# 186 products of the last chunks as two halves of 64 contraction rows, ordered by a semaphore

## The chip, the cores and the metric

The kernel runs on one core of a Trainium2 chip. The metric is device time in microseconds, the median of several runs. Work is done by TensorE (matrix products into the accumulation memory, PSUM), VectorE, ScalarE and GpSimd (elementwise work), and by DMA queues. In the profile they are PE, DVE, ACT, POOL and SP; PEld is TensorE's weight load.

## The reference

Windowed attention with block summaries, then a two-layer network with an ELU between the layers. All of it is in f32.

```python
# attention: q, k, v of (4, 8, 768, 64); 24 blocks of 32 keys; window 16
k_sum = k.reshape(B, H, nb, block, D).max(axis=3)
v_sum = v.reshape(B, H, nb, block, D).mean(axis=3)
scores = [scale * q @ k.T where |i - j| < 16, scale * q @ k_sum.T + log(32)]
a = softmax(scores);  attn = a @ [v, v_sum]
x = attn as (3072 tokens, 512)
# network: w_in (512, 2048), w_out (2048, 512)
h = x @ w_in
g = where(h > 0, h, exp(min(h, 0)) - 1)
out = g @ w_out
```

## The kernel before, in words

The 3072 tokens go in six chunks of 512. A chunk's first layer is 16 blocks of 128 hidden columns, its second layer adds the 16 blocks into four PSUM banks of 128 tokens by 512. Each f32 operand is split into a high and a low part (both float32r), so a product of two f32 matrices is three products on TensorE: high by high, high by low, low by high. "Product" below means one such instruction: a stationary operand of 128 contraction rows by 128 columns and a moving one of 128 rows by 256 or 512 columns.

The change lies in the last two chunks. There the first layer of the last chunk is done by a scheme with seven block products in place of eight (numbered 1 to 7, function `run` inside the loop over eight pairs of hidden blocks, `i` = 0 to 7, `then` holds what is done with each result). Each of the seven takes six TensorE products of 512 columns into one bank (line 788, `seventh`). In the same loop the second layer of the chunk before goes on (`layer2`, line 642).

After that the second layer of the last chunk is done in the same manner (`run_pair`, line 1162, with its products in line 868): seven pairs of hidden blocks, 0 to 6, each of 42 products of 256 columns, six to a block product. Products 1, 6, 7 and 5 have a bank each (`m`, four banks, two token blocks side by side in it). Products 2, 3 and 4 add into the four banks `o`: 2 into the lower columns of the first two, 3 into the upper columns of the same two, 4 into the lower columns of the last two. All seven pairs add into the same places. The order within a pair is 1, 6, 7, 5, 2, 3, 4. Beside it, VectorE and ScalarE prepare the operands of a later pair (`prepare`, `parts`): `token_wholes` adds and subtracts, `token_blocks` (ScalarE line 839, VectorE line 830) and `token_halves` (line 855) split into high and low parts. They have two sets of homes, so the operands for pair i + 2 go where those of pair i lay, and their first write waits for the last product of pair i that reads them.

The order of the instructions on each engine is that in which the code is written out here, one stream an engine. TensorE takes its stream in order; an instruction that waits for a semaphore holds back those behind it.

Of the kernel before, what the change touches and what calls it, by code (L numbers as in the profile page):

```python
# [7 lines left out]

# [2 lines left out]

# [15 lines left out]
P = 128  # L27
# [11 lines left out]
def attn_elu_ffn(ctx: ExitStack, tc: tile.TileContext, qT, kT, vT, v, w_in, w_out, out):  # L39
    nc = tc.nc  # L40
# [10 lines left out]
    NF = DF // P  # L51
# [143 lines left out]
    def x_of(c, part, p):  # L195
        return xs[c][part][p // 2][:, p % 2, :]
# [403 lines left out]
    def fetch(f, tag):  # L600
        weights[(2, f)] = wts.tile([P, 2, WC], F32R, tag=tag, name="w2")
        nc.sync.dma_start(out=weights[(2, f)].bitcast(F32), in_=kept[f])

    def layer1(c, f):
        w = weights[(1, f)]
        h_ps = psum.tile([P, CH], F32, tag="h", name="h", bufs=2)
        parts = ((0, 0), (0, 1), (1, 0))
        runs = [(cc, part) for cc in range(NCC) for part in parts]
        if c == 0:
            runs = [r for r in runs if r[1][0] == 0] + [r for r in runs if r[1][0] == 1]  # L610
        for k, (cc, (a, bb)) in enumerate(runs):
            nc.tensor.matmul(h_ps, w[:, a, cc * P:(cc + 1) * P], x_of(c, bb, cc), start=(k == 0), stop=(k == len(runs) - 1))  # L612
        return h_ps
# [164 lines left out]
    def seventh(i, k, bank):  # L778

        left, right = LEFT[k], RIGHT[k]  # L780
        if left[0] == "a":
            tile, at = weights[(1, 2 * i + int(left[1]) - 1)], 2 * int(left[2]) - 2
        else:
            tile, at = sums_of[i][left]
        runs = [(cc, part) for cc in range(2) for part in ((0, 0), (0, 1), (1, 0))]
        for j, (cc, (a, bb)) in enumerate(runs):
            moving = xs[4][bb][int(right[1]) - 1] if right in ("b11", "b21") else pair[right][bb]
            nc.tensor.matmul(bank, tile[:, a, (at + cc) * P:(at + cc + 1) * P], moving[:, cc, :],  # L788
                             start=(j == 0), stop=(j == len(runs) - 1))

    inner = {}

# [66 lines left out]
    def layer2_seventh(i, k, outs, first, last):  # L859

        left = inner["left", i][k]
        one, two = inner[i]
        low, high = slice(0, WC // 2), slice(WC // 2, WC)
        w1, w2 = (weights[(2, 2 * i + j)] for j in range(2))
        w, cols = {1: (w1, low), 2: (w2, low), 3: (w2, high), 4: (two, low), 5: (one, low), 6: (two, high), 7: (one, high)}[k]
        for s in range(2):
            for j, (a, bb) in enumerate(((0, 0), (0, 1), (1, 0))):
                nc.tensor.matmul(outs[s], left[a][:, s * P:(s + 1) * P], w[:, bb, cols],  # L868
                                 start=first and j == 0 and k != 3 and (s == 0 or k in (2, 4)), stop=last and j == 2 and s == 1)

    def begin_next():

# [90 lines left out]
    with tc.manual_schedule(engines={engines["PE"], engines["SP"]}):  # L963
# [4 lines left out]
        for n in range(NF, 4 * NF):  # L968
# [11 lines left out]
            for b, first in first_at.items():  # L980
                steps = [i for i in range(first - 9, first) if i % NF > 0][:2 * NP]
                if n in steps:
                    i, p = divmod(steps.index(n), NP)
# [76 lines left out]
        for i in range(NF // 2):  # L1060
            p1, u2, u3, u4, e22, e12 = flat[:6]

            def first(ps):
                nc.scalar.copy(out=p1, in_=ps)

            def second(ps):
                add(ps, ps, p1)
                e = exp_of(ps)
                elu(e, ps)
                split(late - 1, 2 * i, e)  # L1070

            def sixth(ps):
                add(u2, ps, p1)

            def last(ps):
                add(u3, ps, u2)

            def fifth(ps):
                add(u4, ps, u2)
                add(ps, ps, u3)  # L1080
                finish(e22, ps)

            def third(ps):
                add(ps, ps, u4)
                finish(e12, ps)

            def fourth(ps):
                add(ps, ps, u3)
                e = exp_of(ps)
                elu(e, ps)  # L1090
                split(late - 1, 2 * i + 1, e, low=nc.vector if i == NF // 2 - 1 else None)

            then = {1: first, 6: sixth, 5: fifth, 2: second, 7: last, 3: third, 4: fourth}

            def run(*ks):
                for k in ks:
                    tag, bufs = (("h", 2), ("a0", 1), ("h", 2), ("a1", 1))[n_seventh[0] % 4]
                    n_seventh[0] += 1
                    ps = psum.tile([P, CH], F32, tag=tag, name="h", bufs=bufs)
                    seventh(i, k, ps)  # L1100
                    then[k](ps)

            if i == 0:
                run(1, 2)
                fetch(0, "w2_0")
                layer2(3, NF - 1)
                fetch(1, "w2_1")
                run(6, 7, 5, 3)
                fetch(2, "w2_4")
                fetch(3, "w2_5")  # L1110
                layer2(late - 1, 0)
                run(4)
            else:
                turn = gs["hi"]
                store(i - 1, 0, e12)
                store(i - 1, 1, e22)
                if i == NF // 2 - 2:
                    fetch_g(0)
                if i == NF // 2 - 1:
                    fetch_inner(0, [(wts, "w2_2"), (wts, "w2_3")])  # L1120
                    fetch_g(1)
                    run(1, 6, 7)
                    with tc.issue_after(turn):
                        list(parts(0))
                    run(5, 2)
                    layer2(late - 1, 2 * i - 1)
                    run(4, 3)
                else:
                    run(1, 6, 7, 5, 2)
                    layer2(late - 1, 2 * i - 1)  # L1130
                    run(3, 4)
                layer2(late - 1, 2 * i)
            if i + 1 < NF // 2:
                weight_sums(i + 1)
            for j in range(2 if i < 6 else 0):
                fetch(2 * i + 4 + j, f"w1_{2 * i + j}")
            if i in last_models:
                m = last_models[i]
                wholes[m] = [ffn.tile([P, WC], F32, tag="cv", name="one", bufs=2) for _ in range(2)]
                for part in range(2):  # L1140
                    model_sums(m, part, *(weights[(2, 2 * m + j)] for j in range(2)))
                model_halves(m, [(att, "xa2"), (att, "xa3")])
                model_store(m)
# [6 lines left out]
    with tc.manual_schedule(engines=set(engines.values())):  # L1150
        ends = (NF - 2, NF - 1)

        def prepare(i):
            list(parts(i))

        half_m = DO // 2
        o_acc[late] = [psum.tile([P, DO], F32, tag=tag, name="o", bufs=bufs) for tag, bufs in (("h", 2), ("h", 2), ("a1", 1), ("a0", 1))]
        outs = {}
        for k, (s, cols) in {2: (0, 0), 3: (0, 1), 4: (2, 0)}.items():
            outs[k] = [o_acc[late][s + j][:, cols * half_m:(cols + 1) * half_m] for j in range(2)]  # L1160

        def run_pair(i, ks=(1, 6, 7, 5, 2, 3, 4)):
            for k in ks:
                layer2_seventh(i, k, outs[k], i == 0, i == NF // 2 - 2 and k not in (2, 3, 4))

        run_pair(0, (2, 4))
        with tc.issue_after(gs["hi"]):
            prepare(1)
        layer2(late - 1, NF - 1)
        banks = {k: psum.tile([P, 2, half_m], F32, tag=f"o{j}", name="m") for j, k in enumerate((1, 6, 7, 5))}  # L1170
        outs.update((k, [t[:, s, :] for s in range(2)]) for k, t in banks.items())
        run_pair(0, (3, 1, 6, 7, 5))
        fetch_g(4)
        fetch_inner(4, [(wts, "w2_0"), (wts, "w2_1")])
        for i in (5, 6, 7):
            fetch_g(i)
        run_pair(1)
        prepare(2)
        fetch_inner(5, [(wts, "w2_2"), (wts, "w2_3")])
        run_pair(2)  # L1180
        prepare(3)
        fetch_inner(6, [(wts, "w2_6"), (wts, "w2_7")])
        run_pair(3)
        prepare(4)
        run_pair(4)
        prepare(5)
        run_pair(5)
        prepare(6)
        for j, f in enumerate(ends):
            split(late, f, g_tiles[NF // 2 - 1][j], wts.tile([P, 2, CH], F32R, tag=f"w1_{12 + j}", name="g"))  # L1190
        run_pair(6)
        shared = [wts.tile([P, 2, DO], F32, tag=f"w2_{4 + j}", name="shared") for j in range(2)]
        m1, u4, u3, v3 = (shared[j][:, :, k * half_m:(k + 1) * half_m] for j in range(2) for k in range(2))
        nc.scalar.copy(out=m1, in_=banks[1])
        add(u3, banks[6], m1)
        add(u4, banks[5], u3)
        add(u3, banks[7], u3)
        add(v3, banks[5], u3)
        layer2_last(late, ends, shared)
# [37 lines left out]
```

## Time and profile before

| | |
|---|---|
| median of 3 runs | 603.74 us (603.58 to 604.01) |
| span of the profiled execution | 601.7 us |
| busy: TensorE | 591.7 us, 98% |
| busy: VectorE, ScalarE, GpSimd | 382.6, 341.5, 346.7 us |
| products of line 868 (256 columns) | 294 |
| products of line 788 (512 columns) | 336 |

The span runs from the first to the last instruction of one execution; the timed runs hold some 2 us more around it. In the timeline a row gives the start and the length of a run of like instructions on one engine. A product's length is modelled and overlaps that of the next: the pitch, from start to start, is what a product takes of TensorE's time.

### The profile page before, as it was taken

Reading aid. Unit: us, or ns where it says so; the run is one execution under the profiler, and the core shown is the slowest. Engines: PE = TensorE matmul, PEld = TensorE weight load, DVE = VectorE, ACT = ScalarE, POOL = GpSimd, SP = SyncE. Lnnn points to the kernel's source line nnn. Section 1 sums busy time; section 2 is a strip of 40 time slices with the busy share of each in tenths; the row PEclk is TensorE's granted clock in tenths of the full one; section 3 lists DMA queues with packets and bytes.
Section 4 is the critical chain, followed back from the end, with each engine's and each line's share of the span. In section 5 each row is a group of like instructions: output and inputs, shape, how many; then the busy total and the mean of one; then the engine's idle time right before and its main releaser. Section 6 shows DMA issues by size and latency. Waiting matters only on the chain.

```text
span 601.7 us, 11834 instructions
## 1 busy us (share of the span) xinstructions
PE 591.7 (98%) x4134; PEld 488.9 (81%) x4134; DVE 382.6 (64%) x1078; ACT 341.5 (57%) x849; POOL 346.7 (58%) x368
## 2 busy tenths in 40 slices
PE   8899999999999999999999999999999999999997
PEld 7678778878888788888887888878888888888997
DVE  7767766647566665657774655666685444459773
ACT  5787777865554345553555645555556555555340
POOL 5778888883332333546578893322668779991001
PEclk9999999999999999999999999999999999999999
DMA  9999979307466566645976565552365233536951
GB/s 328 230 285 308 308 231 296 98 1 272 130 192 214 173 215 217 181 132 174 272 217 214 188 201 178 173 172 73 106 213 171 104 107 103 182 153 243 377 202 71
DMA packets 90092, 115.90 MB, mean 193 GB/s; under 512 B 31409, under 2 KB 67505, under 8 KB 90033
## 3 DMA queue, kind: packets, MB, share of 16 engines
q1 hardware_dynamic: 87296, 110.29, 58.4%
q10 hardware_dynamic: 2736, 4.85, 2.2%
q8 instruction: 33, 0.54, 0.4%
q14 instruction: 27, 0.21, 0.1%
HBM read 88.11 MB, written 26.21 MB: 190 GB/s over the span
## 4 chain that ended last, share of the span: by engine, by line
PE 84%; DMA 7%; DVE 4%; ACT 1%; SPq 1%; issue 1%; POOL 1%; DVEq 0%; POOLq 0%
PE o L642 32%; PE h L612 25%; PE h L788 11%; PE m L868 3%; PE o_ps L175 3%; PE s L543 2%; PE o L868 2%; DMA raw_w<-in_w_out_dram 2%; PE s L366 2%; DMA vw<-vs 1%; DMA vw<-in_v_dram 1%; DMA qbd<-in_qT_dram 1%; DMA n<-in_kT_dram 1%; PE o L677 1%; PE idle L303 1%
## 5 line engine op out<-in xcount | busy, mean ns | idle before, releaser
L612 PE MATMUL h<-x,w 128*128 128x512 f32 x768 | 188.7, 394 | 0.0
L630 POOL TENSOR_TENSOR gl<-e,gh 128x512 fp32r<-128x512 f32 x79 | 102.2, 1294 | 127.3 <-ACT gh L629 87.9
L612 PEld LDWEIGHTS h<-x,w 128*128 128x128 f32 x768 | 141.7, 188 | 31.5 <-issue 2.4
L642 PE MATMUL o<-w,gh 128*128 128x512 f32 x640 | 164.7, 392 | 0.0
L642 PEld LDWEIGHTS o<-w,gh 128*128 128x128 f32 x640 | 118.9, 188 | 26.0 <-ACT gh L629 0.8
L623 DVE SCALAR_TENSOR_TENSOR e<-e,h 128x512 f32<-128x512 f32 x80 | 54.9, 686 | 58.9 <-ACT e L619 55.0
L618 ACT ACTIVATE e<-h 128x512 f32<-128x512 f32 x80 | 47.4, 593 | 75.1 <-PE h L612 66.5
L642 PE MATMUL o<-w,gl 128*128 128x512 f32 x320 | 88.1, 389 | 0.8 <-POOL gl L630 0.8
L571 DVE STREAM_TRANSPOSE pt<-sm 32x256 f32<-32x256 f32 x192 | 83.7, 436 | 4.2 <-POOL sm L162 1.5
L153 ACT ACTIVATE sm<-sm,mx 128x120 f32<-128x120 f32 x192 | 73.2, 383 | 19.8 <-DVE mx L145 19.5
L162 POOL TENSOR_TENSOR sm<-sm,r 128x480 f32<-128x480 f32 x48 | 47.8, 996 | 58.0 <-DVE r L161 38.4
L629 ACT CAST gh<-e 128x512 fp32r<-128x512 f32 x80 | 49.6, 619 | 55.0 <-DVE e L623 53.4
L642 PEld LDWEIGHTS o<-w,gl 128*128 128x128 f32 x320 | 60.0, 188 | 13.7 <-POOL gl L630 1.2
L619 ACT ACTIVATE e<-e 128x512 f32<-128x512 f32 x80 | 50.6, 632 | 2.1
L129 POOL TENSOR_TENSOR w<-cv,w 128x512 fp32r<-128x512 f32 x32 | 41.3, 1290 | 5.5 <-ACT w L127 2.6
L145 DVE CUSTOM_DVE_ANT_0 sm<-s,mask 128x120 f32<-128x120 f32 x192 | 41.2, 276 | 0.4 <-PE s L366 0.4
L153 ACT ACTIVATION_READ_ACCUMULATOR sm<-sm,mx 128x1 f32 x192 | 35.9, 187 | 0.0
L120 DVE SCALAR_TENSOR_TENSOR sh<-sh,raw_w 128x512 uint32<-128x512 uint32 x32 | 22.3, 697 | 19.7 <-POOL w L129 9.8
L788 PE MATMUL h<-t,sums 128*128 128x512 f32 x144 | 33.9, 389 | 0.0
L788 PEld LDWEIGHTS h<-t,sums 128*128 128x128 f32 x144 | 27.0, 188 | 5.6
L123 DVE SCALAR_TENSOR_TENSOR cv<-raw_w,sh 128x512 uint32<-128x512 uint32 x32 | 22.0, 688 | 10.9 <-POOL w L129 9.8
L175 PEld LDWEIGHTS o_ps<-pt,vw 120*64 120x64 f32 x640 | 20.6, 137 | 8.5 <-issue 6.0
(147 smaller groups left out, 783.9 us busy)
## 6 DMA issues: line engine op xcount, KB each, us to landing
w<-kept SPq DMA_DIRECT2D x48, 512.0 KB, 4.1
raw_w<-in_w_in_dram SPq DMA_DIRECT2D x16, 512.0 KB, 5.6
raw_w<-in_w_out_dram SPq DMA_DIRECT2D x16, 512.0 KB, 4.2
kept<-w SPq DMA_DIRECT2D x16, 512.0 KB, 3.4
inner<-model SPq DMA_DIRECT2D x14, 512.0 KB, 6.0
model<-inner SPq DMA_DIRECT2D x12, 512.0 KB, 7.1
qbd<-in_qT_dram SPq DMA_DIRECT2D x32, 128.0 KB, 2.8
out_dram<-ots ACTq DMA_DIRECT2D x16, 256.0 KB, 3.9
```

Source lines behind the costliest of these rows:

```text
L129: nc.gpsimd.tensor_tensor(out=w[:, 1, :], in0=cv, in1=w[:, 0, :].bitcast(F32), op=ALU.subtract)
L153: nc.scalar.activation(out=sm[:, t, :], in_=sm[:, t, :], func=AF.Exp, bias=mx[:, t, :], scale=-1.0, accum_out=z[:, t, 0:1])
L162: nc.gpsimd.tensor_tensor(out=sm, in0=sm, in1=r.broadcast_to([P, UW, KC]), op=ALU.mult)
L571: nc.vector.transpose(pt2[j * BLK:(j + 1) * BLK, :, a * BLK:(a + 1) * BLK], sm2[a * BLK:(a + 1) * BLK, :, j * BLK:(j + 1) * BLK])
L612: nc.tensor.matmul(h_ps, w[:, a, cc * P:(cc + 1) * P], x_of(c, bb, cc), start=(k == 0), stop=(k == len(runs) - 1))
L618: nc.scalar.activation(out=e, in_=h_ps, func=AF.Relu, scale=-1.0)
L619: nc.scalar.activation(out=e, in_=e, func=AF.Exp, scale=-1.0)
L623: top = nc.vector.scalar_tensor_tensor(out=e, in0=e, scalar=-1.0, in1=h_ps, op0=ALU.add, op1=ALU.max)
L629: gs["hi"] = nc.scalar.copy(out=gh, in_=e).ins
L630: last = (low or nc.gpsimd).tensor_tensor(out=gl, in0=e, in1=gh.bitcast(F32), op=ALU.subtract)
L642: nc.tensor.matmul(o_acc[c][s], a[:, s * P:(s + 1) * P], w[:, bb, :], start=first and f == 0, stop=last and f == NF - 1)
L788: nc.tensor.matmul(bank, tile[:, a, (at + cc) * P:(at + cc + 1) * P], moving[:, cc, :], start=(j == 0), stop=(j == len(runs) - 1))
```

## The change

A product of 128 contraction rows is sent as two products of 64 rows, an upper half (rows 0 to 63) and a lower half (rows 64 to 127), which add into the same place of the same bank. The lower half is issued eight products behind its upper half: first eight or so upper halves, then upper and lower in turn, and at the end the eight lower halves left. So while both are under way they work on different banks. Where one kind of half opens a run of products in a bank, it waits for a semaphore that the other kind raised at the end of its run there; the semaphore is TensorE's own.

It is done at two places: for block products 1, 6 and 7 of pair 4 of the first layer (18 products of 512 columns), and for pairs 1 to 4 of the second layer (168 products of 256 columns), through which the lag runs on without a break. The order of the seven in a pair of the second layer is now 1, 6, 7, 5, 2, 4, 3.

```diff
+    row_sem = tc.alloc_semaphore("rows")
+    signalled = [0]
+    waiting, told = [], {}
+    def half_rows(item, r, again):
+        o, left, right, first, last, begins, ends = item
+        rows = slice(r * (P // 2), (r + 1) * (P // 2))
+        made = nc.tensor.matmul(o, left[rows], right[rows], start=first and r == 0, stop=last and r == 1)
+        bank = o.tensor.name
+        if begins and (bank, 1 - r) in told:
+            made.wait_op(row_sem, told[bank, 1 - r], "sem-ge")
+        if ends and (r == 0 or again):
+            nc.tensor.drain(fusable=True).then_inc(row_sem, 1)
+            signalled[0] += 1
+            told[bank, r] = signalled[0]
+    def by_halves(items, lag, end, after=None):
+        banks = [item[0].tensor.name for item in items]
+        new = [n == 0 or banks[n] != banks[n - 1] for n in range(len(items))] + [True]
+        items = [(*item, new[n], new[n + 1]) for n, item in enumerate(items)]
+        for item in items + (lag * [None] if end else []):
+            if item:
+                half_rows(item, 0, after is None)
+                waiting.append(item)
+            if len(waiting) > lag or not item:
+                done = waiting.pop(0)
+                half_rows(done, 1, after is None)
+                if after and done[-1]:
+                    after.pop(0)()
...
-                    run(1, 6, 7, 5, 2)
+                    run(1, 6, 7, rows=i == 4)
+                    run(5, 2)
...
-        def run_pair(i, ks=(1, 6, 7, 5, 2, 3, 4)):
+        def run_pair(i, ks=(1, 6, 7, 5, 2, 4, 3)):
...
+        def run_rows(i, end=False):
+            by_halves(run_pair(i), 8, end)
-        run_pair(1)
+        run_rows(1)
         prepare(2)
...
-        run_pair(4)
+        run_rows(4, True)
         prepare(5)
-        run_pair(5)
+        whole(run_pair(5))
```

`seventh` and `layer2_seventh` now return a list of products, which `whole` issues as before. `run` hands the list and the follow-up of each block product to `by_halves` where `rows` is set. `drain(fusable=True).then_inc` puts the signal on the product before it where that one carries none yet. In the built program there are 83 signals: 74 stand on a product, and 9 are drain instructions of their own, behind a product that already carries TensorE's signal to the other engines (two of the nine at the very end of pair 4's lower halves).

TensorE at the start of the first place, before: `h_5715` is the bank of product 1, `h_5723` that of product 6 (numbers tell buffers apart).

```order
L788 MATMUL h_5715<-x_3730,w1_8_1258 128x512 [waits DVE_49]
L788 MATMUL h_5715<-x_3732,w1_8_1258 128x512
L788 MATMUL h_5715<-x_3730,w1_8_1258 128x512 x2
L788 MATMUL h_5715<-x_3732,w1_8_1258 128x512
L788 MATMUL h_5715<-x_3730,w1_8_1258 128x512
L788 MATMUL h_5723<-t2_4587,sums_5703 128x512 [waits DVE_49]
L788 MATMUL h_5723<-t2_4588,sums_5703 128x512
L788 MATMUL h_5723<-t2_4587,sums_5703 128x512 x2
L788 MATMUL h_5723<-t2_4588,sums_5703 128x512
L788 MATMUL h_5723<-t2_4587,sums_5703 128x512
```

And in the changed kernel, where line 614 is the half product and `h_5716` the bank of product 6:

```order
L614 MATMUL h_5715<-x_3730,w1_8_1258 128x512 [waits DVE_49]
L614 MATMUL h_5715<-x_3732,w1_8_1258 128x512
L614 MATMUL h_5715<-x_3730,w1_8_1258 128x512 x2
L614 MATMUL h_5715<-x_3732,w1_8_1258 128x512
L614 MATMUL h_5715<-x_3730,w1_8_1258 128x512
L614 MATMUL h_5716<-t2_4587,sums_5703 128x512 [waits DVE_49]
L614 MATMUL h_5716<-t2_4588,sums_5703 128x512
L614 MATMUL h_5716<-t2_4587,sums_5703 128x512
L614 MATMUL h_5715<-x_3730,w1_8_1258 128x512 [waits rows]
L614 MATMUL h_5716<-t2_4587,sums_5703 128x512
L614 MATMUL h_5715<-x_3732,w1_8_1258 128x512
L614 MATMUL h_5716<-t2_4588,sums_5703 128x512
```

Nine upper halves go ahead; the first lower half of product 1 stands as the tenth, waits for `rows`, and from there upper and lower halves alternate.

TensorE in pair 1 of the second layer, before: the last of product 5 (`m_6332`), then product 2 into banks `o_6277` and `o_6278`, and product 3 into the upper columns of the same two.

```order
L868 MATMUL m_6332<-model_6260,sums_6303 128x256 x2
L868 MATMUL m_6332<-model_6260,sums_6304 128x256
L868 MATMUL m_6332<-model_6260,sums_6303 128x256 x2
L868 MATMUL m_6332<-model_6260,sums_6304 128x256
L868 MATMUL o_6277<-w2_5292,sums_6297 128x256 x2
L868 MATMUL o_6277<-w2_5292,sums_6298 128x256
L868 MATMUL o_6278<-w2_5292,sums_6297 128x256 x2
L868 MATMUL o_6278<-w2_5292,sums_6298 128x256
L868 MATMUL o_6277<-w2_5292,sums_6303 128x256 x2
L868 MATMUL o_6277<-w2_5292,sums_6304 128x256
L868 MATMUL o_6278<-w2_5292,sums_6303 128x256 x2
L868 MATMUL o_6278<-w2_5292,sums_6304 128x256
```

And in the changed kernel, where those two banks are `o_6298` and `o_6299`, `m_6353` is product 5's bank and `o_6301` a bank of product 4; `sums_6318` and `sums_6319` belong to product 2, `sums_6324` and on to product 3:

```order
L614 MATMUL o_6300<-model_6282,sums_6319 128x256
L614 MATMUL o_6298<-w2_5292,sums_6318 128x256 [waits rows]
L614 MATMUL o_6301<-model_6282,sums_6318 128x256
L614 MATMUL o_6298<-w2_5292,sums_6318 128x256
L614 MATMUL o_6301<-model_6282,sums_6318 128x256
L614 MATMUL o_6298<-w2_5292,sums_6319 128x256
L614 MATMUL o_6301<-model_6282,sums_6319 128x256
L614 MATMUL o_6299<-w2_5292,sums_6318 128x256 [waits rows]
L614 MATMUL o_6298<-w2_5292,sums_6324 128x256 [waits rows]
L614 MATMUL o_6299<-w2_5292,sums_6318 128x256
L614 MATMUL o_6298<-w2_5292,sums_6324 128x256
L614 MATMUL o_6299<-w2_5292,sums_6319 128x256
```

The first upper half of product 3 into `o_6298` waits for `rows`, and stands three instructions behind the last lower half of product 2 into that bank.

## Rows read from the trace of the kernel before

**Rows 1.** The page: its head, TensorE's busy time, granted clock, the chain's shares

```profile
span 601.7 us, 11834 instructions
...
PE 591.7 (98%) x4134; PEld 488.9 (81%) x4134; DVE 382.6 (64%) x1078; ACT 341.5 (57%) x849; POOL 346.7 (58%) x368
...
PEclk9999999999999999999999999999999999999999
...
PE 84%; DMA 7%; DVE 4%; ACT 1%; SPq 1%; issue 1%; POOL 1%; DVEq 0%; POOLq 0%
```

**Rows 2.** Who TensorE waited for, 480 to 602 us: total us, times, longest

```profile
PE o L868 <- DVE vw L623: 0.2, 1, 0.2
```

**Rows 3.** Timeline of TensorE, 494.4 to 500.2 us: start us, length us

```profile
494.46 1.52 PE L788 MATMUL h<-x,w 128*128 128x512 f32 x6
495.82 4.24 PE L788 MATMUL h<-t,sums 128*128 128x512 f32 x18
499.90 0.62 PE L788 MATMUL h<-x,w 128*128 128x512 f32 x2
```

**Rows 4.** Timeline of TensorE, 567.3 to 572.7 us

```profile
567.58 0.88 PE L868 MATMUL m<-w,sums 128*128 128x256 f32 x6
568.30 2.32 PE L868 MATMUL m<-model,sums 128*128 128x256 f32 x18
570.46 1.60 PE L868 MATMUL o<-w,sums 128*128 128x256 f32 x12
571.90 0.88 PE L868 MATMUL o<-model,sums 128*128 128x256 f32 x6
572.62 0.28 PE L868 MATMUL m<-w,sums 128*128 128x256 f32 x1
```

**Rows 5.** Groups of TensorE instructions by shape: count, busy us, mean ns

```profile
L788 PE MATMUL h<-t,sums 128*128 128x512 f32 x144 | 33.9, 389 | 0.0
...
L543 PE MATMUL s<-kw,qbd 64*64 64x120 f32 x512 | 16.8, 269 | 0.9 <-DVE x L202 0.9
L868 PE MATMUL m<-model,sums 128*128 128x256 f32 x126 | 16.3, 283 | 0.0
...
L533 PE MATMUL s<-kw,qbd 128*128 128x120 f32 x64 | 8.6, 277 | 0.5 <-DVE x L202 0.5
```

**Rows 6.** Timeline of TensorE, 135.4 to 136.3 us

```profile
135.19 0.59 PE L543 MATMUL s<-kw,qbd 64*64 64x120 f32 x16
135.71 0.96 PE L612 MATMUL h<-x,w 128*128 128x512 f32 x3
```

**Rows 7.** Timeline of TensorE, 97.9 to 99.0 us

```profile
98.04 1.05 PE L533 MATMUL s<-kw,qbd 128*128 128x120 f32 x8
```

**Rows 8.** Timeline of all engines, 567.3 to 568.2 us

```profile
567.46 0.79 PEld L868 LDWEIGHTS m<-w,sums 128*128 128x128 f32 x6
...
567.70 0.93 ACT L839 CAST sums<-g 128x256 fp32r<-128x256 f32 x2 [2.52 <-PE o L868]
```

**Rows 9.** Timeline of TensorE, 554.2 to 556.3 us

```profile
555.38 0.98 PE L868 MATMUL o<-model,sums 128*128 128x256 f32 x6 [0.19 <-DVE vw L623]
556.20 0.40 PE L642 MATMUL o<-w,gh 128*128 128x512 f32 x1
```

**Rows 10.** Timeline of VectorE, 567.3 to 572.7 us

```profile
568.14 1.22 DVE L830 TENSOR_TENSOR sums<-g,sums 128x256 fp32r<-128x256 f32 x2 [0.23 <-ACT sums L839]
569.61 1.23 DVE L830 TENSOR_TENSOR sums<-pt,sums 128x1024 fp32r<-128x1024 f32 x1 [0.26 <-ACT sums L855]
```

More of the change, by code (lines that the diff above doesn't have):

```diff
@@ L10 @@
 from contextlib import ExitStack
+from functools import partial
 import concourse.bass as bass
@@ L602, in fetch, with whole @@
         nc.sync.dma_start(out=weights[(2, f)].bitcast(F32), in_=kept[f])
+    row_sem = tc.alloc_semaphore("rows")
[25 more added lines that the diff above has]
+                    after.pop(0)()
+    def whole(items):
+        for o, left, right, first, last in items:
+            nc.tensor.matmul(o, left, right, start=first, stop=last)
     def layer1(c, f):
@@ L785, in seventh @@
         runs = [(cc, part) for cc in range(2) for part in ((0, 0), (0, 1), (1, 0))]
+        items = []
         for j, (cc, (a, bb)) in enumerate(runs):
             moving = xs[4][bb][int(right[1]) - 1] if right in ("b11", "b21") else pair[right][bb]
-            nc.tensor.matmul(bank, tile[:, a, (at + cc) * P:(at + cc + 1) * P], moving[:, cc, :],
-                             start=(j == 0), stop=(j == len(runs) - 1))
+            items.append((bank, tile[:, a, (at + cc) * P:(at + cc + 1) * P], moving[:, cc, :], j == 0, j == len(runs) - 1))
+        return items
     inner = {}
@@ L865, in layer2_seventh @@
         w, cols = {1: (w1, low), 2: (w2, low), 3: (w2, high), 4: (two, low), 5: (one, low), 6: (two, high), 7: (one, high)}[k]
[L866 to L869, printed above, removed]
+        return [(outs[s], left[a][:, s * P:(s + 1) * P], w[:, bb, cols],
+                 first and j == 0 and k != 3 and (s == 0 or k in (2, 4)), last and j == 2 and s == 1)
+                for s in range(2) for j, (a, bb) in enumerate(((0, 0), (0, 1), (1, 0)))]
     def begin_next():
@@ L1093, in attn_elu_ffn, with run @@
             then = {1: first, 6: sixth, 5: fifth, 2: second, 7: last, 3: third, 4: fourth}
-            def run(*ks):
+            def run(*ks, rows=False):
+                products, after = [], []
                 for k in ks:
@@ L1099, in run @@
                     ps = psum.tile([P, CH], F32, tag=tag, name="h", bufs=bufs)
-                    seventh(i, k, ps)
-                    then[k](ps)
+                    items = seventh(i, k, ps)
+                    if rows:
+                        products += items
+                        after.append(partial(then[k], ps))
+                    else:
+                        whole(items)
+                        then[k](ps)
+                if rows:
+                    by_halves(products, 8, True, after)
             if i == 0:
@@ L1160, in attn_elu_ffn @@
             outs[k] = [o_acc[late][s + j][:, cols * half_m:(cols + 1) * half_m] for j in range(2)]
-        def run_pair(i, ks=(1, 6, 7, 5, 2, 3, 4)):
-            for k in ks:
-                layer2_seventh(i, k, outs[k], i == 0, i == NF // 2 - 2 and k not in (2, 3, 4))
-        run_pair(0, (2, 4))
+        def run_pair(i, ks=(1, 6, 7, 5, 2, 4, 3)):
+            return [item for k in ks for item in layer2_seventh(i, k, outs[k], i == 0, i == NF // 2 - 2 and k not in (2, 3, 4))]
+        whole(run_pair(0, (2, 4)))
         with tc.issue_after(gs["hi"]):
@@ L1171, in attn_elu_ffn @@
         outs.update((k, [t[:, s, :] for s in range(2)]) for k, t in banks.items())
-        run_pair(0, (3, 1, 6, 7, 5))
+        whole(run_pair(0, (3, 1, 6, 7, 5)))
         fetch_g(4)
@@ L1176, in attn_elu_ffn @@
             fetch_g(i)
-        run_pair(1)
+        def run_rows(i, end=False):
+            by_halves(run_pair(i), 8, end)
+        run_rows(1)
         prepare(2)
         fetch_inner(5, [(wts, "w2_2"), (wts, "w2_3")])
-        run_pair(2)
+        run_rows(2)
         prepare(3)
         fetch_inner(6, [(wts, "w2_6"), (wts, "w2_7")])
-        run_pair(3)
+        run_rows(3)
         prepare(4)
-        run_pair(4)
+        run_rows(4, True)
         prepare(5)
-        run_pair(5)
+        whole(run_pair(5))
         prepare(6)
@@ L1190, in attn_elu_ffn @@
             split(late, f, g_tiles[NF // 2 - 1][j], wts.tile([P, 2, CH], F32R, tag=f"w1_{12 + j}", name="g"))
-        run_pair(6)
+        whole(run_pair(6))
         shared = [wts.tile([P, 2, DO], F32, tag=f"w2_{4 + j}", name="shared") for j in range(2)]
```

## Prediction

> **What bounds the kernel now.** I read the page's head and busy table first, then the chain, then who TensorE waits for, then TensorE's timeline at the two places of the change. TensorE is busy 98% of the span at the full granted clock (the level of 2.4 GHz), and 84% of the chain that ended last is TensorE [rows 1]. From 480 us to the end it waits for another engine once, for 0.2 us [rows 2]. So a nanosecond added to or taken from TensorE's stream at the places of the change is one in the kernel's time, unless a later wait takes it in, and there is none.
>
> What is to be seen in the timeline is the pitch, the time from one product's start to the next, and not the duration. The first place is pair 4 of the first layer: product 1 starts at 494.46 us, products 6, 7 and 5 follow, and product 2 starts at 499.90, so 24 products take 5.44 us, 0.227 each, and the 18 that are halved take 4.08 [rows 3]. A pair of chunks in the last layer is 42 products of 256 columns, from 567.58 to 572.62 us: 5.04 us, 0.120 each [rows 4]. At 2.4 GHz, 512 columns take 0.213 us and 256 take 0.107. So a whole product costs about 0.013 us beyond its columns, whatever its length. That is all that the change can win: 186 x 0.0133 = 2.5 us.
>
> **The slots of the halves.** A half has 64 rows but as many columns, so it streams as long as the whole product; nothing is won unless an upper and a lower half run side by side. That two row groups can is shown in plain f32: in the score products the tiles of 64x64 come four to a set, two row groups by two column groups. Sixteen of them take 0.59 us with the last one's 0.27 in it, so three steps of four take 0.32 us, 0.10 to 0.11 a set [rows 5, 6], while one whole product of the same 120 columns takes (1.05 - 0.28) / 7 = 0.111 [rows 5, 7]. So a set in tiles costs at most about 0.008 us less than one whole product. No row shows float32r halves of 64x128. Bounds for a slot (one upper with one lower): 0.107 to 0.120 for 256 columns, 0.213 to 0.227 for 512. I take the nearest row's gain of 0.008: 0.112 and 0.219.
>
> The lag of eight has a price of its own. In the first eight slots only upper halves run, in the last eight only lower ones, so n products take n + 8 slots. First place: 26 x 0.219 = 5.69 us in place of 4.08, +1.6 (bounds 26 x 0.213 and 26 x 0.227: +1.5 to +1.8). Second place, where the lag runs on over four pairs: 176 x 0.112 = 19.71 in place of 168 x 0.120 = 20.16, -0.45 (bounds -1.3 to +1.0). Entering and leaving the tile mode: from the last set of tiles to the first whole product the trace has 135.71 - 135.51 = 0.20 us where a set takes 0.10 [rows 6], so 0.1 a change, four changes, +0.4 (0.2 of it at each place).
>
> **The signals.** No row shows a product of this engine waiting for another of its own at this distance, so the price comes from neighbours. A product lasts 0.283 us [rows 5]. A ScalarE cast that waits for the last but one product of a pair (start 567.34) begins at 567.70 [rows 8], so from start to the waiter's start 0.28 to 0.36; I take 0.34. After a wait the weight load stands bare: after the one wait in these rows six products take 0.82 us from start to next start, where 6 x 0.120 is 0.72, so 0.10 [rows 9]. Together 0.44 us from the start of the product waited for to the start of the one that waits. Whatever stands behind it on TensorE, the other half's products too, waits as well, since the engine takes them in order; nobody else is waited for.
>
> Who waits with less than 0.44 us of its own? (a) Product 3's upper halves go into the banks of product 2, whose lower halves end three instructions earlier, one to two slots, 0.11 to 0.22 us. So 0.22 to 0.33 is lost, twice a pair, eight times: I take 0.23 each, +1.85 (bounds 0 if the signal comes at once, 2.6). The new order 2, 4, 3 only lengthens this distance. (b) The lower half that opens a bank of six stands three slots behind the signal, 0.34 us: about 0.1 lost once a pair, after which the lower stream hangs back by that much and finds the next signals there: +0.4 (0 to 1.6). In the first place three slots are 0.66 us, a 512-column product lasts 0.389 [rows 5], and nothing is lost. (c) Nine of the 83 signals can't ride on their product, which already carries one, and stand as drains. If a drain lets nothing start until the products before it have ended, the next starts 0.44 us after the last instead of 0.11 later, 0.33 lost; if it costs no more than a signal that rides, 0; its whole point is to tell of an end, so I take 0.30, +2.7 (0 to 3.0).
>
> The Trainium skill, page "PSUM — Partial Sum Buffer", section "Engine vs sequencer instructions", says that a drain waits for the engine to go fully idle. By it the upper end holds, 9 x 0.33 = 3.0. No row of this trace shows a drain between products.
>
> Other engines: VectorE and ScalarE prepare the pair after next. The last write of it in this stretch ends at 570.84 and the first use is at 572.62 or later, so 1.8 us of slack [rows 4, 10]; the lag lets go of the old operands some 8 x 0.11 = 0.9 us later. That hides; without the cover it would cost the difference. The additions after products 1, 6 and 7 come up to eight slots later, but products 5 and 2 fill a fresh bank and the one that product 1 has left, 12 x 0.227 = 2.7 us of work in which TensorE needs none of them. No DMA is moved.
>
> **Sum.** First place +1.6 + 0.2; second -0.45 + 0.2 + 1.85 + 0.4 + 2.7: in all +6.5 us. The profiled execution spans 601.7 us and the timed median is 603.74, the rest lying around the span and untouched. 603.74 + 6.5 = 610.2.
>
> **Rivals.** Signals free: row groups run side by side, and signals and drains cost nothing. Then the lag and the mode decide: +1.6 + 0.4 and -1.3 to 0 in the second place, 604.4 to 605.8, say 604.9. For it: signals on products cost nothing in the pitch of 0.227 today. Against it: in (a) the distance is shorter than the product itself, which lasts 0.283.
>
> Faster: the lone halves at the ends are overlapped with the whole products around them, and each half's weight load hides behind the other row group. Then only columns count: 168 x 0.0133 + 18 x 0.0133 = 2.5 us less, 601.3. It decides if the pitch over the lone eight falls toward half. Against it: lone uppers share one row group, and weight loads are already under way beside the products (six in 0.79 us from 567.46, [rows 8]). The Trainium skill, "TensorE: Matmul & The Clock Gate", Part 3, says that a weight load overlaps a running matmul only when their row groups differ; by that rule the 0.013 is load time and this rival's 2.5 us are there to win. The trace disagrees as far as it goes: [rows 8] shows loads beside products of the same rows.
>
> No concurrency: float32r halves run one after the other. Then 168 x 0.120 + 18 x 0.227 come on top, +24.2, 628. Against it: the sets of [rows 6].
>
> **Chances.** Forecast 0.63 (its own range 607 to 613), signals free 0.18, faster 0.10, no concurrency 0.09. 0.2% of 603.74 is 1.2 us, about what a measurement tells from no change. The free-signal case lies on both sides of 604.95: a third of it, 0.06, is "same". Slower: 0.63 + 0.09 + 0.11 = 0.83; faster 0.10, with 0.01 of the free-signal case 0.11. The range must hold the forecast and the free signals: 603.5 to 613.0; outside it remain "faster", "no concurrency" and little else.
>
> **What would show it.** Right: upper-half pitch near 0.11 in the middle of a run of the second place, gaps of about 0.44 us from start to start at each drain and of 0.33 or more at the opening of product 3, the first place some 5.7 us long, eight lone halves at either end. Wrong: no gap at a drain or at product 3 (signals free), a pitch of 0.24 for an upper and a lower together (no concurrency), or lone halves at under their column time (faster).

## The result, and the profile after

The changed kernel takes 612.46 us (612.15 to 613.75, four runs) against 603.78 for the kernel before, run beside it: 8.7 us more, a ratio of 1.0146 (95% interval 1.0132 to 1.0161). The forecast was slower, 610.2, with a range of 603.5 to 613.0. Direction and range held, the range by 0.5 us at its upper end; the loss is 2.2 us larger than forecast.

The page of the changed kernel, its head, TensorE's busy time, granted clock and the chain's shares, answers to [rows 1]:

```profile
span 612.0 us, 12224 instructions
...
PE 600.6 (98%) x4320; PEld 493.2 (81%) x4320; DVE 382.4 (62%) x1078; ACT 341.6 (56%) x849; POOL 346.9 (57%) x368
...
PEclk9999999999999999999999999999999999999999
...
PE 88%; POOL 3%; DVE 3%; DMA 2%; ACT 1%; issue 1%; SPq 0%; PEldq 0%; PEld 0%; DVEq 0%; POOLq 0%; ACTq 0%
```

TensorE's 8.9 us more of busy time are nearly the whole loss; the clock is full throughout, VectorE, ScalarE and GpSimd do what they did. So nearly all of the loss is in TensorE's own stream, as the forecast had it. The span is 10.3 us longer, but 1.5 us of that were there before the first halved product, 1.3 of them already at 16 us of the execution, in a stretch where the two programs are alike; 8.8 us remain and agree with the timed 8.7.

The groups of TensorE instructions by shape (count, busy us, mean ns) show that a half is not a cheaper instruction: 64 rows by 256 columns last 283 to 297 ns, 64 rows by 512 columns 388 to 409; the whole ones lasted 283 and 389 [rows 5].

```profile
L614 PE MATMUL o<-w,sums 64*128 64x256 f32 x96 | 14.5, 297 | 0.1
L614 PE MATMUL m<-model,sums 64*128 64x256 f32 x144 | 14.2, 283 | 0.3
...
L614 PE MATMUL h<-t,sums 64*128 64x512 f32 x24 | 4.6, 388 | 0.0
...
L614 PE MATMUL h<-x,w 64*128 64x512 f32 x12 | 3.3, 409 | 0.0
```

The first place in the timeline of TensorE (start us, length us), which answers to [rows 3]:

```profile
496.03 1.65 PE L614 MATMUL h<-x,w 64*128 64x512 f32 x6
497.52 0.39 PE L614 MATMUL h<-t,sums 64*128 64x512 f32 x1
497.74 0.50 PE L614 MATMUL h<-x,w 64*128 64x512 f32 x1
497.76 0.62 PE L614 MATMUL h<-t,sums 64*128 64x512 f32 x2
498.08 0.40 PE L614 MATMUL h<-x,w 64*128 64x512 f32 x1
498.22 0.39 PE L614 MATMUL h<-t,sums 64*128 64x512 f32 x1
498.32 0.39 PE L614 MATMUL h<-x,w 64*128 64x512 f32 x1
498.45 0.39 PE L614 MATMUL h<-t,sums 64*128 64x512 f32 x1
...
499.13 3.03 PE L614 MATMUL h<-t,sums 64*128 64x512 f32 x17
502.09 1.20 PE L640 MATMUL h<-t,sums 128*128 128x512 f32 x4
```

Read it in two columns. `h<-x,w` begins as the upper halves of product 1, and from 497.74 on these are its lower halves; `h<-t,sums` are the upper halves of products 6 and 7 and, in the row of 499.13, their lower halves too. From 498.08 a lower half starts every 0.23 us and an upper half every 0.23 us: the two row groups do run side by side. But neither stream is faster than whole products were (0.227), and at both ends one stream is alone. From the first half to the next whole product 6.06 us pass, where 18 whole products took 4.08. The first lower half, the tenth in the program, starts at 497.74, 0.45 us after the start of the sixth upper half, whose signal it waits for, and ahead of the eighth and ninth upper halves.

The second place, in the middle of pair 2, which answers to [rows 4]:

```profile
577.22 0.28 PE L614 MATMUL o<-w,sums 64*128 64x256 f32 x1
577.26 0.28 PE L614 MATMUL o<-model,sums 64*128 64x256 f32 x1
577.34 0.28 PE L614 MATMUL o<-w,sums 64*128 64x256 f32 x1
577.38 0.28 PE L614 MATMUL o<-model,sums 64*128 64x256 f32 x1
...
577.58 0.83 PE L614 MATMUL o<-w,sums 64*128 64x256 f32 x6
578.14 0.28 PE L614 MATMUL o<-model,sums 64*128 64x256 f32 x1
578.36 0.38 PE L614 MATMUL o<-w,sums 64*128 64x256 f32 x1
578.36 0.38 PE L614 MATMUL o<-model,sums 64*128 64x256 f32 x1
578.58 0.28 PE L614 MATMUL o<-w,sums 64*128 64x256 f32 x1
...
578.93 0.28 PE L614 MATMUL m<-w,sums 64*128 64x256 f32 x1
578.94 0.28 PE L614 MATMUL o<-model,sums 64*128 64x256 f32 x1
579.32 0.38 PE L614 MATMUL m<-w,sums 64*128 64x256 f32 x1
579.33 0.38 PE L614 MATMUL o<-w,sums 64*128 64x256 f32 x1
579.54 0.28 PE L614 MATMUL m<-w,sums 64*128 64x256 f32 x1
```

Three things stand in these rows. In the first four, `o<-w` (one row group) and `o<-model` (the other) each start every 0.120 us, 0.04 apart: side by side, at the pitch of whole products. The run from 577.58 on and the row of 578.36 are the openings of product 3's two banks; from 578.14 the starts go on in steps of 0.22, to 578.36 and 578.58, where 0.12 is usual. From 578.93 to 579.32 lies a drain: 0.39 to the next start, then 0.22 where 0.12 is usual. The whole place takes 26.27 us from its first half (566.60) to the next whole product (592.87), where the same four pairs took 20.16.

### The profile page after: what moved, and what is told of

It reads as the page before. It is cut to its first block, busy times and chain, and to the rows that moved or that the text cites. A ratio compares the mean times of both kernels' runs of the same rounds, so it can differ in the third digit from the quotient of the medians.

```text
span 612.0 us, 12224 instructions
## 1 busy us (share of the span) xinstructions
PE 600.6 (98%) x4320; PEld 493.2 (81%) x4320; DVE 382.4 (62%) x1078; ACT 341.6 (56%) x849; POOL 346.9 (57%) x368
## 4 chain that ended last, share of the span: by engine, by line
PE 88%; POOL 3%; DVE 3%; DMA 2%; ACT 1%; issue 1%; SPq 0%; PEldq 0%; PEld 0%; DVEq 0%; POOLq 0%; ACTq 0%
PE o L680 33%; PE h L650 26%; PE h L640 12%; PE o_ps L176 3%; PE m L614 3%; PE s L544 3%; PE m L640 1%; PE o L614 1%; DMA kw<-in_kT_dram 1%; PE o L640 1%; POOL w L130 1%; PE h L614 1%; PE o L715 1%; POOL sm L163 1%; DMA v<-in_v_dram 1%
## 5 line engine op out<-in xcount | busy, mean ns | idle before, releaser
L640 PE MATMUL h<-t,sums 128*128 128x512 f32 x132 | 31.4, 390 | 0.0
L640 PEld LDWEIGHTS h<-t,sums 128*128 128x128 f32 x132 | 24.7, 188 | 5.4 <-issue 0.4
```

Of the source, the lines that this page charges most:

```text
L640: nc.tensor.matmul(o, left, right, start=first, stop=last)
```

## The experiments

Each was timed in three rounds beside the kernel before, which took 604.15 us in the first four and 604.02 in the other four. Line 614 is 615 in some of them, and 640 is 652.

**The first place alone.** The second place goes as whole products in the new order 2, 4, 3.

```diff
-            by_halves(run_pair(i), 8, end)
+            whole(run_pair(i))
```

> Only the first place is halved (18 products of 512 columns), the second place goes whole, in the new order. Lag theory: 18 products take 26 slots of 0.227 us, plus the change of mode: 6.1 us in place of 4.08, +2.0, and about 0.3 more where later work waits for results that come eight slots later: 605.9 to 606.2. Rival, signals alone cost (there is no drain here and no signal that comes late): 603.8 to 604.0.

Measured 606.42, +2.3 us, ratio 1.0041 (1.0026 to 1.0056). The price of the lag is there although all but its ends runs side by side.

**The second place alone.**

```diff
-                    run(1, 6, 7, rows=i == 4)
+                    run(1, 6, 7)
```

> Only the second place is halved (168 products of 256 columns, 9 drains). If the two places add up: the whole change is +8.7, the first place 2.1 to 2.4 of it, so +6.3 to 6.6 here: 610.1 to 610.4. Rival, the two places share a cost (later work that waits for the first place only): under 609 or over 611.

Measured 610.55, +6.4, ratio 1.0105 (1.0090 to 1.0120). 2.3 and 6.4 are 8.7, so the two places add up. The place is 26.27 us long again.

**The order alone.** No halves, only 2, 4, 3 for 2, 3, 4.

```diff
-                    run(1, 6, 7, rows=i == 4)
+                    run(1, 6, 7)
...
-            by_halves(run_pair(i), 8, end)
+            whole(run_pair(i))
```

> No halves at all, only the order 1, 6, 7, 5, 2, 4, 3 in the pairs of the second layer. Lag and signal theory: 603.8, no change. Rival, the order itself holds up the operands of a later pair or the last additions: over 604.5.

Measured 604.07, ratio 1.0002 (0.9993 to 1.0012): the order costs nothing.

**No drains.** The second place alone. Every lower half that ends a run in a bank gives its `rows` signal with the next lower half, so that none falls on a product that already carries TensorE's signal to the others; only product 2's two a pair give it at once, since product 3 waits for them.

```diff
+        if r == 1 and later:
+            tell(later.pop())
...
+        if ends and r == 1 and again:
+            if n_low[0] % 10 in (5, 6):
+                tell(bank)
+            else:
+                later.append(bank)
```

> As the second place alone, but the signals that stood as drains ride on the next lower half, so there is no drain of its own. Signal theory: in the changed kernel's trace a drain costs 0.36 to 0.44 us against the pitch, 9 of them 3.7, so +2.6 is left: 606.4. Rival, the gaps at the drains are waits for operands that VectorE prepares too late, since the lag lets go of their homes later: the gaps stay, 610.

Measured 607.49, +3.3, ratio 1.0057 (1.0042 to 1.0072): 3.1 us less than with the nine drains. The place is 23.11 us long, so the nine were worth 26.27 - 23.11 = 3.16, 0.35 each. That is less than the 3.7 expected, so that +3.3 is left and not +2.6; the rival, that the gaps stay, falls. At the spot in its timeline where a drain stood, two starts every 0.11 us go on; the steps at product 3 stay:

```profile
568.33 0.28 PE L615 MATMUL o<-model,sums 64*128 64x256 f32 x1
568.55 0.38 PE L615 MATMUL o<-w,sums 64*128 64x256 f32 x1
568.56 0.38 PE L615 MATMUL o<-model,sums 64*128 64x256 f32 x1
568.78 0.28 PE L615 MATMUL o<-w,sums 64*128 64x256 f32 x1
...
569.12 0.28 PE L615 MATMUL m<-w,sums 64*128 64x256 f32 x1
569.13 0.28 PE L615 MATMUL o<-model,sums 64*128 64x256 f32 x1
569.24 0.28 PE L615 MATMUL m<-w,sums 64*128 64x256 f32 x1
```

**Product 2 far from product 3.** The second place alone, with the drains, in the order 1, 2, 6, 7, 3, 5, 4: twelve products stand between the last of product 2 and the first of 3. Fewer signals collide there, so five drains are left.

```diff
-            by_halves(run_pair(i), 8, end)
+            by_halves(run_pair(i, (1, 2, 6, 7, 3, 5, 4)), 8, end)
```

> The second place alone, with the order 1, 2, 6, 7, 3, 5, 4 in the halved pairs, so that product 3 opens its banks twelve products after product 2; five drains are left. Signal theory: eight waits of 0.21 us go (-1.65), four drains of 0.42 go (-1.7): 0.96 for the lag, 0.2 for the mode, 2.1 for the drains, +3.3: 607.1. Rival, product 3's gaps only move to another wait: about 608.7 or more.

Measured 607.61, +3.6, ratio 1.0055 (1.0038 to 1.0072), the place 23.20 us long. The steps of 0.22 away from drains are gone.

**Both: far and no drains.** The order of the last kernel, and every lower half's signal with the next lower half, product 2's too.

```diff
+            if False:
+                tell(bank)
+            else:
+                later.append(bank)
...
-            by_halves(run_pair(i), 8, end)
+            by_halves(run_pair(i, (1, 2, 6, 7, 3, 5, 4)), 8, end)
```

> The second place alone, far order, no drain of its own. Lag theory: only the lag is left, 176 slots of 0.120 in place of 168, +0.96, and 0.2 for the mode: 604.9 to 605.1. Rival, the halves themselves cost something each (336 of them, with 79 signals): 606 or more. Rival, without waits the side by side halves gain 0.008 a slot as predicted: 603.5.

Measured 605.35, +1.3, ratio 1.0016 (1.0005 to 1.0028). The place is 21.37 us long, and its timeline has no gap left but at the ends, here the entry, two slots of the middle, and the exit:

```profile
561.80 0.88 PE L652 MATMUL m<-model,sums 128*128 128x256 f32 x6
562.61 0.97 PE L615 MATMUL m<-w,sums 64*128 64x256 f32 x6
...
566.74 0.28 PE L615 MATMUL o<-w,sums 64*128 64x256 f32 x1
566.78 0.28 PE L615 MATMUL m<-model,sums 64*128 64x256 f32 x1
566.86 0.28 PE L615 MATMUL o<-w,sums 64*128 64x256 f32 x1
566.90 0.28 PE L615 MATMUL m<-model,sums 64*128 64x256 f32 x1
...
583.17 0.88 PE L615 MATMUL o<-model,sums 64*128 64x256 f32 x6
583.98 0.98 PE L652 MATMUL m<-w,sums 128*128 128x256 f32 x6
```

The signals are still there, 79 of them, each on a product. With product 3's waits and the drains gone, what is left is the lag and the change of mode, and no gain from 168 products going side by side. By differences of the places' lengths the five drains of the kernel with product 2 far cost 23.20 - 21.37 = 1.83, 0.37 each, and the eight waits of the kernel without drains 23.11 - 21.37 = 1.74, 0.22 each.

**Half as many products.** The kernel just told, with halves in pairs 1 and 2 alone, 84 products. Were something paid or won per product, this should halve what is left.

```diff
-        run_rows(2)
+        run_rows(2, True)
...
-        run_rows(3)
+        whole(run_pair(3))
...
-        run_rows(4, True)
+        whole(run_pair(4))
```

> As the far order without drains, but only pairs 1 and 2 are halved, 84 products in place of 168. Lag theory: the cost belongs to the two ends, not to the products, so it stays at +1.1 to +1.2: 604.9 to 605.0. Rival, each half costs or gains something: half of what 168 products cost.

Measured 605.60, +1.6, ratio 1.0023 (1.0012 to 1.0034). The place is 11.29 us long against 2 x 5.04 = 10.08 before: +1.21, as the 168 had 21.37 - 20.16 = +1.21. The cost belongs to the ends and does not grow with the number of products. This rests on the places' lengths; the times alone, 0.2 us above the kernel with twice as many, can't tell it, and 605.60 is 0.6 above what was expected, within the interval.

**The first place with a lag of 16.** Everything else as in the first experiment.

```diff
-                    by_halves(products, 8, True, after)
+                    by_halves(products, 16, True, after)
```

> The first place alone with a lag of sixteen in place of eight. Lag theory: eight more slots of 0.227, +1.8 over the first place with a lag of eight: 607.6 to 608. Rival, lone halves of one kind run faster than a pair or overlap with what stands around them: under 607.

Measured 607.44, +3.4, ratio 1.0051 (1.0030 to 1.0071): only 1.1 more than with a lag of 8, not 1.8, and neither the expected time nor the rival's. The timeline says why:

```profile
493.98 1.65 PE L614 MATMUL h<-x,w 64*128 64x512 f32 x6
495.47 1.99 PE L614 MATMUL h<-t,sums 64*128 64x512 f32 x8
497.09 0.50 PE L614 MATMUL h<-x,w 64*128 64x512 f32 x1
...
498.57 2.88 PE L614 MATMUL h<-t,sums 64*128 64x512 f32 x12
501.38 1.66 PE L640 MATMUL h<-t,sums 128*128 128x512 f32 x6
```

In program order 17 upper halves stand ahead of the first lower one. By the start times it comes beside the fourteenth, at 497.09: a lower half starts ahead of three upper halves that stand before it. So the lone stretch is shorter than the lag. And what is said ahead of the prediction, that TensorE takes its stream in order, does not hold between the two row groups when nothing waits. With a lag of 8 the first lower half has to wait for the signal of the sixth upper half and starts beside the eighth. The place takes 7.41 us with 16 and 6.08 with 8, 1.33 more for eight steps of lag in place of 8 x 0.227 = 1.8. A further 0.5 us in the profile of the kernel with lag 8, late results told below, is not in the profile of this one, which brings 1.33 down to about 0.9. That the rest of the miss lies within the timing's interval is likely; it wasn't tested, and neither was a longer lag at the second place.

## Why the prediction was right, point by point

The mechanism was right: the lag, the changes of mode, product 3's waits and the drains make the loss, in TensorE's own stream. The sizes were less so. The terms that were too small or left out lack 2.8 us together, and 0.5 us was charged too much in (a) and (b); that these partly cancel is luck.

The lengths of the places split the loss by differences between kernels. The terms, forecast against measured:

| term | forecast us | measured us | from |
|---|---|---|---|
| first place, slots | +1.6 | +1.8 | 6.06 - 4.08, plus 0.20 in the steps next to it, less the mode |
| second place, slots | -0.45 | +1.0 | 21.37 - 20.16, plus 0.19 next to it, less the mode |
| changes of mode, four | +0.4 | +0.8 | entry and exit steps, below |
| (a) product 3's waits, 8 | +1.85 | +1.74 | 23.11 - 21.37 |
| (b) lower halves that open a bank | +0.4 | 0 | no gap left in the kernel far and without drains |
| (c) drains, 9 | +2.7 | +3.16 | 26.27 - 23.11 |
| late results after the first place | 0 | +0.3 | starts of the same products before and after, below |
| sum | +6.5 | +8.8 | timed +8.7 |

**What bounds.** Right: every one of these shows in full in the time, and all but the late results arise in TensorE's own stream.

**Slots: the term that was most mis-sized.** The forecast took from the f32 score tiles that a slot of an upper and a lower half costs 0.008 us less than a whole product. It costs the same: 0.120 at 256 columns, 0.227 to 0.232 at 512. The upper bounds held exactly. Each row group's stream keeps the 0.013 us beyond the columns; running two streams side by side doesn't share it out. The reading of [rows 6] itself was right: in those products sets of four tiles start at 134.98, 135.08, 135.19 and 135.29 us, 0.103 apart, against 0.111 for a whole product of the same columns. What failed is carrying it over, from plain f32 in tiles of 64x64, with two column groups as well, to float32r halves of 64x128. Which of these differences matters no run shows. With 0.120 and 0.227 the slots would have been 176 x 0.120 - 20.16 = +0.96 and 26 x 0.227 - 4.08 = +1.8, as measured. This term is the largest part of the miss, 1.6 of 2.3 us.

**Mode.** Also too small. At entry and exit two steps are lengthened, not one: in the first place 0.32 and 0.34 in place of 0.227 each, in the second 0.21 and 0.22 in place of 0.120 each, so 0.19 to 0.20 a change. The forecast read one step in [rows 6] and stopped there; the second stands in the same rows, three products in 0.96 us where 2 x 0.227 and a length of 0.39 are 0.84.

**Waits on its own signals.** (a) was right in size and in its parts. In the kernel without drains the last lower half of product 2 in its first bank starts at 567.65 and the waiting product at 567.99, 0.34 us, and the step after it is 0.22, some 0.10 too long: the 0.34 and 0.10 of the forecast. Both row groups are held up by it, as forecast, and each wait shows as two steps of 0.22 in place of 0.12, so 0.2 lost, where the forecast took 0.23. (b) was charged for nothing: in the kernel far and without drains no gap is left. Where product 3 waits, the lower stream hangs back by 0.08 us once in each later pair while the upper one goes on at 0.12; what that may cost is in the 1.74 of (a).

**Drains.** Just above the upper bound of 3.0: 0.35 to 0.37 each, where the bound took 0.33 and the sum 0.30. The 0.10 for the step after (0.22) is as forecast; what was too small is the gap itself, 0.38 to 0.39 us from start to start where the forecast had 0.34. The nearer answer was the rule of the Trainium skill, "PSUM — Partial Sum Buffer", section "Engine vs sequencer instructions", that a drain waits for the engine to go idle. The trace agrees: 0.38 to 0.39 us from the last start ahead of a drain to the next one, more than a product's 0.28.

**Other engines.** A term put at nothing that measured 0.3. At 510.58 TensorE's weight load waits for ScalarE's cast of `gh`. Before, in ScalarE's rows, that cast came well ahead of its use at 506.70, and the cast of `sums`, which waits for GpSimd, stood behind it:

```profile
504.67 0.62 ACT L629 CAST gh<-e 128x512 fp32r<-128x512 f32 x1 [0.83 <-DVE e L623]
505.20 0.62 ACT L773 CAST sums<-one 128x512 fp32r<-128x512 f32 x1
```

In the changed kernel the cast of `sums` stands ahead of the exponentials that lead to `gh`, and holds ScalarE up for 4.39 us:

```profile
506.15 0.62 ACT L811 CAST sums<-one 128x512 fp32r<-128x512 f32 x1 [4.39 <-POOL one L800]
...
509.91 0.62 ACT L667 CAST gh<-e 128x512 fp32r<-128x512 f32 x1 [0.82 <-DVE e L661]
...
510.58 0.76 PEld L680 LDWEIGHTS o<-w,gh 128*128 128x128 f32 x4 [0.44 <-ACT gh L667]
```

So the forecast asked when the results come, but not in what order ScalarE takes its work. The order is the new one in the three kernels traced with a halved first place, and the old one in those with the second place or the order alone; why it moved, no run shows. It is 0.3 us in the stream of products, and 0.13 follow at 527.49, where a weight load waits for GpSimd's `gl`, by the starts of the same products in both traces; 0.17 come back at the one wait of [rows 2], which no longer occurs. With a lag of 16 the cast of `gh` ends as long after the first half as with 8, 14.5 us, but TensorE comes to it 1.3 us later, and so doesn't wait. This is read from the traces; no run puts the old order back.

**The rivals.** "No concurrency" falls by the timeline and the two experiments without drains. "Faster" falls: the lone halves take 0.117 to 0.121 and 0.22 to 0.24 a step, what whole products take, and nothing is won between. By the rule of the Trainium skill's page "TensorE: Matmul & The Clock Gate", Part 3, weight loads that alternate between row groups should have hidden what didn't hide before; the trace disagrees with what the prediction drew from it, the slot is 0.120 either way. Whether the 0.013 is load time at all, no run shows. "Signals free" falls by the experiment without drains and by the one with product 2 far, each of which gives back about 3 us.

## What to carry to other kernels

Splitting a full-height product into row-group halves won nothing here, where the pitch of whole products is already their columns plus 0.013 us: the halves stream as many columns, each row group pays the same 0.013, and the lag, the two changes of mode and the signals come on top. A saving read from neighbouring rows of another type and tile shape is a bound, not a forecast: 0.008 us a set was real in the f32 score tiles and nothing was left of it in float32r halves. Look along each engine's stream for an instruction that has moved ahead of what the next stage waits for; here a cast did. Where one engine must signal itself, count the instructions between signal and waiter, and put a signal that finds its instruction taken on the next one instead of a drain: that took back 3.1 of 6.4 us without moving a product.

## What the runs showed of the hardware that was not expected

- A product in one row group can start ahead of products of the other row group that stand before it in the program: with a lag of 16, three places ahead (497.09 us, beside the fourteenth upper half), with a lag of 8 two (497.74 us).
- Two row groups of 64x128 in float32r run fully side by side (starts 0.04 us apart at a pitch of 0.120 each), yet a pair in a slot is no quicker than one whole product of 128 rows.
- A change between whole products and halves lengthens two steps by about 0.1 us each, at 256 and at 512 columns alike.
- A drain that stands alone costs 0.35 to 0.37 us of TensorE's time; a wait on its own signal three instructions on costs 0.22, and holds up both row groups.
